# One row in eight of the query weights loaded over other queues: 112 rows on SP, two rows in sixteen parts, fourteen rows in two-row DMAs from GpSimd

## Chip, core and metric

The kernel runs on one NeuronCore of a Trainium2 chip. The metric is device time in microseconds (us), the median over runs; every time is that of one execution of the whole program. A core has four compute engines: TensorE (PE; its weight loads are PEld), VectorE (DVE), ScalarE (ACT) and GpSimd (POOL). SyncE (SP) here only issues DMAs. Sixteen DMA engines move all data between HBM and the core's memory (SBUF), whichever queue a DMA was issued on. A DMA is split into packets over these engines, and it has landed when the last of them is done.

## The reference

One decode step of a block that adds attention over a cache and a token-mixing MLP to its input. Batch 8, one token, width 512; 32 query heads share 8 key/value heads; 8192 cached positions of 128 numbers; float32 throughout.

```python
xn = _layernorm(x)
q = (xn @ wq).reshape(B, 1, 32, 128)                  # wq: 512 x 4096
scores = einsum(q, repeat(k_cache, 4)) * 128 ** -0.5
o = einsum(softmax(scores), repeat(v_cache, 4))
A = o.reshape(B, 1, 4096) @ wo                        # wo: 4096 x 512
h = _layernorm(xn)
u = gelu(einsum("bsd,sf->bdf", h, w1) + b1)           # 1792 features, S = 1
Bm = einsum("bdf,fs->bds", u, w2) + b2
return x + A + Bm.transpose(0, 2, 1)
```

Keys and values are 268 MB each, `wq` and `wo` 8.4 MB each. Every byte of them is used once.

## The kernel before

Work goes by pairs of one key/value head and one batch entry, `N_IT` = 64 in all. A pair has one key load (`raw<-in_A_k_cache_dram`) and one value load of 4 MB each. A load fills one of five slots (`RING`) of the tile `raw`: 128 partitions with 32 KB in each. `load_next` (L87) takes the next load from a list, `order`, and issues it on SP's queue; it is called as soon as the program has written the last use of a slot, so SP stands there until that use is over. All loads of the stream go through this one queue, in the list's order. The first key load is cut into four pieces of 8 KB a partition, and the last value load into five (`PIECES`), followed by the last part of `wo` in four pieces (L109).

For one pair, VectorE turns the keys in place in four quarters (`turn_keys`, L259), TensorE multiplies them with the placed queries (`qk`, L270), the softmax goes over VectorE, TensorE and ScalarE (L282 to L322), and TensorE multiplies with the values (`pv`, L337, and L347 for the last pair). `pair(i)` interleaves the keys of pair i, the scores of i-1 and the values of i-2. Between them ScalarE and GpSimd carry the MLP in 112 small steps (`mx_step`, L427 to L429), which read `w1t`, `b1t` and `w2t`. The last three pairs are written out by hand at the end, followed by the output projection `y_add` (L411), which reads the last part of `wo`, and the store of the result.

At the start the query weights `wq` come first on SP's queue. They take two slots: 128 partitions with 64 KB each, every partition one contiguous row of 64 KB in HBM (L83). Three loads follow at once: two of keys and one of values. The projection `q_project` (L224, matmuls at L230) reads all of `wq`; after it the two slots are free, and the next key and value load are issued. Before the projection stand the two layer norms, and a matmul (L218) that needs `b2t` through L210.

GpSimd's queue carries four small loads at the start: `w1t`, `b1t`, `w2t` (128 rows of 56 bytes each) and `b2t` (8 rows of 4 bytes). ACT's queue carries the input `x`. Near the end, in the last fifteen turns of the main loop, SP also issues a small DMA into `pad`, of 15 rows of 16 bytes in the first of these turns and one row less in each after it (L490). Nothing reads `pad`.

DMAs signal completion through semaphores, eight for SP's and ACT's queues together (`DMAHW0` to `DMAHW7`) and eight for GpSimd's (`DMASW0` to `DMASW7`), used in turn. A DMA whose semaphore is still in use by an earlier one waits for that one to land.

Of the kernel before, what the change touches and what calls it, by code (L numbers as in the profile page):

```python
# [14 lines left out]
B, D, HQ, HKV, SK, DH, F = 8, 512, 32, 8, 8192, 128, 1792  # L15
REP = HQ // HKV
P = 128
# [7 lines left out]
NC = D // P  # L25
# [3 lines left out]
N_IT = B * HKV  # L29
# [11 lines left out]
def attn_mixer_kernel(ctx: ExitStack, tc: tile.TileContext, x, kc, vc, wq, wo, w1, b1, w2, b2, out):  # L41
    nc = tc.nc
    place = ctx.enter_context(tc.tile_pool(name="place", bufs=1))
    pad = place.tile([P, PAD // 4], F32, name="pad")
# [4 lines left out]
    def slot(n=1):  # L49
        at = taken[0] % RING  # L50
        taken[0] += n
        return slots[:, at:at + n, :]
# [11 lines left out]
    def misc():  # L64
        return ps_m.tile([P, 512], F32, name="misc")
# [11 lines left out]
    at = [o[1:] for o in order].index((kc, KR, N_IT - 1))  # L77
    order[at], order[at + 1] = order[at + 1], order[at]
    WQ = []

    def load_wq():
        t = slot(2).rearrange("p s m -> p (s m)")
        nc.sync.dma_start(t, wq.rearrange("(p c) n -> p (c n)", c=NC))  # L83
        t = t.rearrange("p (c n) -> p c n", c=NC)
        WQ.extend(t[:, c, :] for c in range(NC))

    def load_next():  # L87
        if order:
            _, src, to, i = order.pop()
            h, b = divmod(i, B)  # L90
            t = slot().rearrange("p s (t d) -> p (s t) d", d=DH)
            rows = src[b, h].rearrange("(p t) d -> p t d", p=P)
            first, last = to is KR and not i, not order
            at = 0
            for n in (CH_T,) * NCH if first else PIECES if last else (NT,):
                nc.sync.dma_start(t[:, at:at + n, :], rows[:, at:at + n, :])
                at += n
            to[i] = t
            if last:
                load_wo(HKV - 1)  # L100
# [3 lines left out]
    def load_wo(h):  # L104
# [7 lines left out]
        wos[h] = t  # L112

    load_wq()
    early = one.tile([P, HB, 512], F32, name="ob")
    x_sb = early[:B, 0, :]
    nc.scalar.dma_start(x_sb, x.rearrange("b s d -> (b s) d"))
    w1t = const.tile([P, NF], F32, name="w1t")
    b1t = const.tile([P, NF], F32, name="b1t")
    w2t = const.tile([P, NF], F32, name="w2t")  # L120
    b2t = const.tile([B, 1], F32, name="b2t")
    yrow = const.tile([W, D], F32, name="yrow")
    for _ in range(RING - 2):
        load_next()
    nc.gpsimd.dma_start(w1t, w1.rearrange("s (p c) -> p (s c)", p=P))
    nc.gpsimd.dma_start(b1t, b1.rearrange("(p c) -> p c", p=P))
    nc.gpsimd.dma_start(w2t, w2.rearrange("(p c) s -> p (c s)", p=P))
    nc.gpsimd.dma_start(b2t, bass.AP(tensor=b2.tensor, offset=b2.offset, ap=[[0, B], [1, 1]]))
    quarter = [slice(j * D // NB, (j + 1) * D // NB) for j in range(NB)]


    ident = const.tile([P, P], F32, name="ident")
    make_identity(nc, ident)

# [46 lines left out]
    for k in range(NPT):  # L183
        t = const.tile([P, CH_T * W + W], F32, name=f"pt{k}")
# [3 lines left out]
    for k in range(2):  # L188
        t = const.tile([P, REP, W], F32, name=f"ot{k}")
        nc.gpsimd.memset(t, 0.0)  # L190
        OTS.append(t)


    def layer_norm(dst, src):
# [18 lines left out]
    m = misc()  # L213
# [3 lines left out]
    m = misc()  # L217
# [6 lines left out]
    def q_project():  # L224
        for a in range(2):
            m = misc()
            for c in range(NC):
                for g in range(HKV // 2):
                    o = (a * HKV // 2 + g) * REP * DH
                    nc.tensor.matmul(m[g * W:(g + 1) * W, :], xnT[:, c, :], WQ[c][:, o:o + REP * DH],  # L230
                                     start=(c == 0), stop=(c == NC - 1))
# [3 lines left out]
            for r in range(REP):  # L235
                nc.tensor.transpose(mt[:, r * P:(r + 1) * P], q[:, r * DH:(r + 1) * DH], ident)
            nc.vector.tensor_copy(QT[:, a * HKV // 2:(a + 1) * HKV // 2].rearrange("p g b r -> p r g b"),
                                  mt.rearrange("p (r g b) -> p r g b", r=REP, b=W)[:, :, :, :B])
        WQ.clear()
        load_next()  # L240
# [198 lines left out]
    def pair(i):  # L439
        h, b = divmod(i, B)  # L440
        k, v = i - 1, i - 2
        mb, mj = divmod(2 * (i - 1), NF)
        mixing = 0 <= mb < B
        turn_keys(i, 0)
        if k >= 0:
            qk(k)
        if v > 0:
            o_place(v - 1)
        if b == 0:
            q_place(h)  # L450
        turn_keys(i, 1)
        if k >= 0:
            sm_max(k)
            sm_spread(k)
        if v >= 0:
            pv(v, 0)
        if mixing:
            if mj == 0:
                if mb:
                    mx_end(mb - 1)  # L460
                mx_begin(mb)
            mx_step(mb, mj)
        if mb == B and mj == 0:
            mx_end(B - 1)
        turn_keys(i, 2)
        if k >= 0:
            sm_bias(k)
            sm_exp(k)
        if v >= 0:
            pv(v, 1)  # L470
            o_take(v)
        turn_keys(i, 3)
        if k >= 0:
            sm_send(k)
            if k >= N_IT - B:
                sm_sum(k)
            sm_turn(k)
        if mixing:
            mx_step(mb, mj + 1)
        if b == 3 and h:  # L480
            o_project(h - 1)
        if b == 3 and h < HKV - 1:
            load_wo(h)

    spare = pad[:16, :60].rearrange("p (n k) -> p n k", k=4)
    for i in range(N_IT - 2):
        pair(i)
        n = N_IT - 3 - i
        if 0 < n < 16:
            nc.sync.dma_start(spare[:n, n - 1, :], wo[:n, :4])  # L490


    k = N_IT - 1
# [88 lines left out]
```

## Time and profile before

| | |
|---|---|
| median of 3 runs | 1295.35 us (1294.91 to 1295.48) |
| the profiled execution, its own time | 1294.88 us |
| its span, first to last instruction | 1293.1 us |
| busy: PE / DVE / ACT / POOL | 829.3 / 726.9 / 331.2 / 229.6 us |
| read from HBM | 553.69 MB, 428 GB/s over the span |
| granted TensorE clock, mean | 0.818 |

The profile is of one execution. Its page has busy times, the span in 40 slices with the busy share of the 16 DMA engines, the DMA queues, the chain of waits followed back from the last instruction, and the costliest groups of instructions. q1 is SP's queue, q10 ACT's, q0 GpSimd's; q8 and q14 carry instructions, which the engines fetch while they run. A view of chosen stretches of time gives each engine's busy time in it (with the count of instructions), the granted clock, and the DMA share and rate. The timeline lists instructions as start, duration, engine, line, operation and names; in square brackets stands how long the engine was idle before, and what ended it. Engines are not told apart within the DMA share.

### The profile page before, as it was taken

How to read it: one execution, taken by the hardware profiler on the slowest of the kernel's cores; microseconds unless marked ns; L12 is line 12 of the kernel's file. 1: busy time of each engine (PE TensorE's matmuls, PEld its weight loads, DVE VectorE, ACT ScalarE, POOL GpSimd, SP SyncE). 2: the span in 40 equal slices, each digit the busy share in tenths (PEclk: the TensorE clock that was granted, in tenths of full speed). 3: DMA queues.
4: the chain of work that ended last, by engine and by line, in shares of the span. 5: the costliest groups of instructions: out<-in, count | busy, mean ns of one | idle time of the engine just before them, and what ended most of it. 6: DMA issues, size and time to landing. Idle time of an engine off the chain costs nothing.

```text
span 1293.1 us, 11759 instructions
## 1 busy us (share of the span) xinstructions
PE 829.3 (64%) x4890; PEld 244.5 (19%) x4890; DVE 726.9 (56%) x648; ACT 331.2 (26%) x479; POOL 229.6 (18%) x247
## 2 busy tenths in 40 slices
PE   2664766756757656666657576567564774657777
PEld 0111211211211111211112111121121221112223
DVE  2655456565555554654646556556456555556774
ACT  0232323222422313223233132232323232311000
POOL 1112112211212122121121131211211221110000
PEclk9877778878878788787887797787876887878899
DMA  9999999999999999999999999999999999999997
GB/s 407 426 432 436 430 435 432 432 432 434 431 432 433 433 432 431 436 431 430 434 431 433 433 430 435 431 433 433 432 431 431 435 432 428 435 432 430 433 437 315
DMA packets 21640, 554.45 MB, mean 429 GB/s; under 512 B 2732, under 2 KB 2764, under 8 KB 3540
## 3 DMA queue, kind: packets, MB, share of 16 engines
q1 hardware_dynamic: 21444, 553.68, 99.4%
q8 instruction: 38, 0.62, 0.2%
q14 instruction: 14, 0.11, 0.0%
q0 software_dynamic: 128, 0.02, 0.0%
q10 hardware_dynamic: 16, 0.02, 0.0%
HBM read 553.69 MB, written 0.02 MB: 428 GB/s over the span
## 4 chain that ended last, share of the span: by engine, by line
DMA 66%; PE 19%; DVE 14%; issue 1%; ACT 0%; SPq 0%; POOL 0%; ACTq 0%; DVEq 0%; POOLq 0%
DMA raw<-in_A_k_cache_dram 63%; PE acc L337 13%; DVE raw L259 12%; DMA raw<-in_A_v_cache_dram 2%; PE misc L287 2%; DMA b2t<-in_B_b_dram 2%; DVE mr L282 1%; PE acc L270 1%; PE misc L230 1%; PE misc L433 0%; PE misc L387 0%; PE hb L419 0%; PE misc L311 0%; DVE oc L366 0%; PE misc L218 0%
## 5 line engine op out<-in xcount | busy, mean ns | idle before, releaser
L259 DVE STREAM_TRANSPOSE raw<-raw 128x2048 f32<-128x2048 f32 x256 | 583.6, 2295 | 292.1 <-DMA raw<-in_A_k_cache_dram 292.1
L337 PE MATMUL acc<-raw,pt 128*32 128x512 f32 x2016 | 340.2, 829 | 0.0
L287 PE MATMUL misc<-ident,mr 128*128 128x128 f32 x128 | 47.0, 466 | 401.0 <-DVE mr L282 401.0
L270 PE MATMUL acc<-raw,z 128*32 128x512 f32 x2048 | 261.0, 609 | 9.7 <-DVE raw L259 7.6
L428 POOL TENSOR_SCALAR g<-g,w2t 128x512 f32<-128x512 f32 x112 | 77.7, 694 | 789.7 <-ACT g L427 789.7
L304 ACT ACT_TABLE_LOAD x57 | 73.1, 1283 | 333.8 <-DVE nb L293 333.5
L429 POOL TENSOR_TENSOR macc<-macc,g 128x512 f32<-128x512 f32 x112 | 142.3, 1271 | 9.4
L427 ACT ACTIVATE g<-hb,b1t,w1t 128x512 f32<-128x512 f32 x112 | 87.1, 777 | 219.7 <-PE hb L419 127.1
L322 DVE STREAM_TRANSPOSE pt<-misc 128x512 f32<-128x512 f32 x64 | 45.5, 710 | 140.0 <-PE misc L311 140.0
L337 PEld LDWEIGHTS acc<-raw,pt 128*32 128x32 f32 x2016 | 74.9, 145 | 211.5 <-issue 210.3
L287 PEld LDWEIGHTS misc<-ident,mr 128*128 128x128 f32 x128 | 29.4, 285 | 449.3 <-DVE mr L282 449.3
L304 ACT ACTIVATE t2k<-acc,nb 128x512 f32<-128x512 f32 x64 | 44.0, 688 | 233.4 <-DVE nb L293 232.8
L270 PEld LDWEIGHTS acc<-raw,z 128*32 128x32 f32 x2048 | 66.5, 111 | 186.3 <-issue 169.7
L311 PE MATMUL misc<-t2k,send 128*128 128x512 f32 x128 | 76.0, 677 | 23.4 <-ACT t2k L304 23.4
L427 ACT ACT_TABLE_LOAD x57 | 73.1, 1283 | 1.0
L358 ACT COPY ob<-acc 128x512 f32<-128x512 f32 x56 | 32.7, 584 | 98.9 <-PE acc L337 98.9
L387 PE MATMUL misc<-ob,pick 128*128 128x512 f32 x112 | 51.5, 603 | 0.0
L282 DVE TENSOR_REDUCE mr<-acc 128x1 f32<-128x512 f32 x64 | 41.8, 653 | 3.0 <-PE acc L270 3.0
L311 PEld LDWEIGHTS misc<-t2k,send 128*128 128x128 f32 x128 | 19.4, 191 | 78.4 <-issue 40.7
L434 DVE TENSOR_TENSOR yrow<-misc,yrow 32x512 f32<-32x512 f32 x8 | 5.4, 678 | 42.7 <-PE misc L433 42.7
L405 PE MATMUL misc<-wo,ot 128*32 128x512 f32 x56 | 27.0, 629 | 0.0
L421 POOL MEMSET macc<- 128x512 f32 x8 | 4.2, 525 | 116.4 <-PE misc L433 97.2
(90 smaller groups left out, 229.5 us busy)
## 6 DMA issues: line engine op xcount, KB each, us to landing
raw<-in_A_k_cache_dram SPq DMA_DIRECT2D x63, 4096.0 KB
raw<-in_A_v_cache_dram SPq DMA_DIRECT2D x63, 4096.0 KB
wo<-in_A_wo_dram SPq DMA_DIRECT2D x7, 1024.0 KB
raw<-in_A_k_cache_dram SPq DMA_DIRECT2D x4, 1024.0 KB
raw<-in_A_v_cache_dram SPq DMA_DIRECT2D x3, 1024.0 KB
raw<-in_A_v_cache_dram SPq DMA_DIRECT2D x2, 512.0 KB
wo<-in_A_wo_dram SPq DMA_DIRECT2D x4, 256.0 KB
ob<-in_A_x_dram ACTq DMA_DIRECT2D x1, 16.0 KB
```

Of the source, the lines that this page charges most:

```text
L259: nc.vector.transpose(k, k)
L270: nc.tensor.matmul(S[i][c * W:(c + 1) * W, :].rearrange("p (t j) -> p t j", j=W), Z[:, q, b, :], k[:, c * CH_T:(c + 1) * CH_T, q * W:(q + ...
L282: nc.vector.tensor_reduce(mr, S[i], AX.X, ALU.max)
L287: nc.tensor.matmul(m[:, :P], st[i].to_broadcast([P, P]), ident, start=True, stop=True)
L304: nc.scalar.activation(p, S.pop(i), AF.Exp, bias=st[i], scale=SCALE, accum_out=lr)
L311: nc.tensor.matmul(m, send, st[i][0], start=True, stop=True)
L322: nc.vector.transpose(PT[i % NPT][:, :CH_T * W], st.pop(i)[0])
L337: nc.tensor.matmul(O[i][j * W:(j + 1) * W, :].rearrange("p (c d) -> p c d", c=NCH), pt[:, t * W:(t + 1) * W], v[:, t], start=(t < NB), sto ...
L387: nc.tensor.matmul(m.rearrange("p (b d) -> p b d", b=HB), pick[:, c, :], ob[:, :, c * DH:(c + 1) * DH], start=(c == 0), stop=(c == NCH - 1))
L427: nc.scalar.activation(g, hb, AF.Gelu_apprx_tanh, bias=b1t[:, j:j + 1], scale=w1t[:, j:j + 1])
L428: nc.gpsimd.tensor_scalar(g, g, w2t[:, j:j + 1], 1.0, op0=ALU.mult, op1=ALU.mult)
L429: nc.gpsimd.tensor_add(acc, acc, g)
```

## The change

Partition rows 0 to 111 of `wq` stay one DMA on SP's queue. Rows 126 and 127 follow there as one DMA each, cut into sixteen parts of 4 KB. The other fourteen rows are issued from GpSimd's queue by `load_side`, two rows at a time: five DMAs of two whole rows and four of two half rows (`PAIRS` has first row, first and last half). Between some of them stand seven small DMAs of 2 to 15 rows of 16 bytes into `pad` (`BETWEEN`). `b2t` moves from GpSimd's queue to ACT's; `w1t`, `b1t` and `w2t` move behind GpSimd's memsets. The fifteen small DMAs on SP near the end go away.

```diff
     WQ = []
+    OWN = 112
+    SPRAYED = (126, 127)
+    PAIRS = ((112, 0, 2), (114, 0, 2), (116, 0, 1), (118, 0, 2), (120, 0, 2), (116, 1, 2), (122, 0, 2), (124, 0, 1), (124, 1, 2))
+    BETWEEN = {0: 15, 3: 2, 4: 6, 6: 4, 7: 6, 8: 6, 9: 7}
+    side = []
+
+    def load_side():
+        for x in range(len(side) + 1):
+            if x in BETWEEN:
+                n = BETWEEN[x]
+                o = 4 * sorted(BETWEEN).index(x)
+                nc.gpsimd.dma_start(pad[:n, o:o + 4], wq[:n, :4])
+            if x < len(side):
+                nc.gpsimd.dma_start(*side[x])
 
     def load_wq():
         t = slot(2).rearrange("p s m -> p (s m)")
-        nc.sync.dma_start(t, wq.rearrange("(p c) n -> p (c n)", c=NC))
+        rows = wq.rearrange("(p c) n -> p (c n)", c=NC)
+        n = NC * HQ * DH
+        nc.sync.dma_start(t[:OWN], rows[:OWN])
+        for p in SPRAYED:
+            nc.sync.dma_start(t[p:p + 1].rearrange("p (m w) -> p m w", m=16), rows[p:p + 1].rearrange("p (m w) -> p m w", m=16))
+        side.extend((t[p:p + 2, a * n // 2:e * n // 2], rows[p:p + 2, a * n // 2:e * n // 2]) for p, a, e in PAIRS)
...
-    nc.gpsimd.dma_start(w1t, w1.rearrange("s (p c) -> p (s c)", p=P))
-    nc.gpsimd.dma_start(b1t, b1.rearrange("(p c) -> p c", p=P))
-    nc.gpsimd.dma_start(w2t, w2.rearrange("(p c) s -> p (c s)", p=P))
-    nc.gpsimd.dma_start(b2t, bass.AP(tensor=b2.tensor, offset=b2.offset, ap=[[0, B], [1, 1]]))
+    nc.scalar.dma_start(b2t, bass.AP(tensor=b2.tensor, offset=b2.offset, ap=[[0, B], [1, 1]]))
...
     make_identity(nc, ident)
+    load_side()
...
         nc.gpsimd.memset(t, 0.0)
         OTS.append(t)
+    nc.gpsimd.dma_start(w1t, w1.rearrange("s (p c) -> p (s c)", p=P))
+    nc.gpsimd.dma_start(b1t, b1.rearrange("(p c) -> p c", p=P))
+    nc.gpsimd.dma_start(w2t, w2.rearrange("(p c) s -> p (c s)", p=P))
...
-    spare = pad[:16, :60].rearrange("p (n k) -> p n k", k=4)
     for i in range(N_IT - 2):
         pair(i)
-        n = N_IT - 3 - i
-        if 0 < n < 16:
-            nc.sync.dma_start(spare[:n, n - 1, :], wo[:n, :4])
```

What stands on SP's queue at the start of the program, before the change, with what each instruction waits for in brackets (a shape is rows by numbers per row, `x4` four alike in a row):

```order
L83 DMA raw<-in_A_wq_dram 128x16384
L96 DMA raw<-in_A_k_cache_dram 128x2048 x4
L96 DMA raw<-in_A_k_cache_dram 128x8192
L96 DMA raw<-in_A_v_cache_dram 128x8192
L96 DMA raw<-in_A_k_cache_dram 128x8192 [waits DMAHW1_49,DMAHW0_49,PE_49]
```

And with the change, at the same place:

```order
L99 DMA raw<-in_A_wq_dram 112x16384
L101 DMA raw<-in_A_wq_dram 1x16384 x2
L115 DMA raw<-in_A_k_cache_dram 128x2048 x3
L115 DMA raw<-in_A_k_cache_dram 128x2048 [waits DMAHW0_49]
L115 DMA raw<-in_A_k_cache_dram 128x8192 [waits DMAHW1_49]
L115 DMA raw<-in_A_v_cache_dram 128x8192 [waits DMAHW2_49]
```

There are three DMAs in place of one, and with more DMAs the semaphores come round sooner: the second key load (the row of 128x8192) now waits for `DMAHW1`, the semaphore of the 112-row load.

On GpSimd (POOL), before, behind the barrier at the program's start:

```order
L125 DMA w1t<-in_B_w_dram 128x14
L126 DMA b1t<-in_B_b_dram 128x14
L127 DMA w2t<-in_B_w_dram 128x14
L128 DMA b2t<-in_B_b_dram 8x1
masks.py:197 MEMSET ident 128x128
```

With the change, from the end of the making of `ident` on:

```order
L91 DMA pad<-in_A_wq_dram 15x4
L93 DMA raw<-in_A_wq_dram 2x16384 x2
L93 DMA raw<-in_A_wq_dram 2x8192
L91 DMA pad<-in_A_wq_dram 2x4
L93 DMA raw<-in_A_wq_dram 2x16384
L91 DMA pad<-in_A_wq_dram 6x4
L93 DMA raw<-in_A_wq_dram 2x16384
L93 DMA raw<-in_A_wq_dram 2x8192 [waits DMASW0_49]
L91 DMA pad<-in_A_wq_dram 4x4 [waits DMASW1_49]
```

Seven more follow, each waiting for the DMA eight places ahead of it to land; then the memsets, and `w1t`, `b1t` and `w2t`. The first eight are issued without a wait.

On TensorE, the first matmul of the projection, before and then with the change:

```order
L230 MATMUL misc<-raw,ob 32x512 [waits DMAHW1_49,DVE_49]
```

```order
L250 MATMUL misc<-raw,ob 32x512 [waits DMASW5_49,DMASW7_49,DMASW4_49,DMAHW1_49,DMASW3_49,DMAHW3_49,DMASW2_49,DMAHW4_49,DMASW1_49,DVE_49]
```

It waited for one DMA on `wq`; it now waits for the three of SP's queue and for GpSimd's.

## The prediction, made before the changed kernel had run

> **What bounds the kernel now.** I began with the page: span, DMA line, queues, chain of waits.
>
> ```profile
> span 1293.1 us, 11759 instructions
> DMA  9999999999999999999999999999999999999997
> q1 hardware_dynamic: 21444, 553.68, 99.4%
> q8 instruction: 38, 0.62, 0.2%
> q14 instruction: 14, 0.11, 0.0%
> DMA 66%; PE 19%; DVE 14%; issue 1%; ACT 0%; SPq 0%; POOL 0%; ACTq 0%; DVEq 0%; POOLq 0%
> ```
>
> The 16 DMA engines are busy in every slice but the last, and two thirds of the chain is DMA. Beside the 553.68 MB of data the same engines carry instruction fetches: 38 packets on q8, 0.62 MB, so 16 KB each. Next, the busy time by stretches of time: bulk, start, the end microsecond by microsecond.
>
> ```profile
> core 0: us, PE busy (x) PEld busy (x) DVE busy (x) ACT busy (x) POOL busy (x), PEclk, DMA share, GB/s
> 8.00:16.00 8.00, 0.61 (x4) 0.55 (x4) 3.90 (x16) 0.59 (x2) 0.00 (x0) 1.00 0.91 394
> 200.00:1200.00 1000.00, 641.19 (x3692) 186.65 (x3688) 562.40 (x474) 275.65 (x390) 193.37 (x200) 0.81 1.00 432
> 1281.00:1282.00 1.00, 1.00 (x36) 0.73 (x28) 0.41 (x1) 0.00 (x0) 0.00 (x0) 1.00 0.93 377
> 1282.00:1283.00 1.00, 1.00 (x31) 0.78 (x26) 0.97 (x2) 0.00 (x0) 0.00 (x0) 1.00 0.67 277
> 1283.00:1284.00 1.00, 0.97 (x26) 0.68 (x18) 0.46 (x2) 0.00 (x0) 0.00 (x0) 1.00 0.60 246
> 1284.00:1285.00 1.00, 0.88 (x32) 0.81 (x32) 0.17 (x1) 0.00 (x0) 0.00 (x0) 1.00 0.59 236
> 1285.00:1286.00 1.00, 0.84 (x24) 0.38 (x16) 0.00 (x0) 0.00 (x0) 0.00 (x0) 1.00 0.58 225
> 1286.00:1287.00 1.00, 0.36 (x14) 0.35 (x16) 0.00 (x0) 0.00 (x0) 0.00 (x0) 1.00 0.55 201
> 1287.00:1288.00 1.00, 0.59 (x14) 0.32 (x5) 0.29 (x1) 0.00 (x0) 0.00 (x0) 1.00 0.40 156
> 1288.00:1289.00 1.00, 0.74 (x25) 0.59 (x24) 0.17 (x1) 0.00 (x0) 0.00 (x0) 1.00 0.26 100
> ```
>
> In the bulk the share is 1.00 at 432 GB/s: 27 GB/s per engine, so a 64 KB row of the query weights costs its engine 65536 B / 27 = 2.43 us. At the end the engines do not stop together. By 1283 the share has dropped to 0.60, some nine or ten of 16; six or seven are done by about 1282. The others run on to about 1288.8. Every data load gives each engine the same bytes, so the late ones have done something else as well. The fetches are the candidate. This window of 1.2 us holds one:
>
> ```profile
> q8 instruction: 1, 0.02, 4.9%
> ```
>
> 4.9% of 16 engines over 1.2 us is 0.94 us. If eight engines carry the 38, each has 4.75, at least 4.5 us. The gap of 6 to 7 us then means about 1.4 us for a fetch with what it delays (6.5 x 8 / 38), an estimate from these rows.
>
> Last, the chain of waits and the timeline, for whether the end follows the late engines.
>
> ```profile
> 1205.17 23.26 DMA raw<-in_A_k_cache_dram
> 1228.46 2.31 DVE raw L259
> 1259.78 26.83 DMA raw<-in_A_v_cache_dram
> 1286.65 0.65 PE L347 MATMUL acc<-raw,pt 128*32 128x128 f32 x16 [0.64 <-DMA raw<-in_A_v_cache_dram]
> 1289.17 0.16 PEld L411 LDWEIGHTS hb<-wo,ot 128*32 128x32 f32 x8 [0.24 <-DMA wo<-in_A_wo_dram]
> ```
>
> It does. A load counts as landed when its slowest engine is done. VectorE waits for a key load until 1228.46; the compute from there runs almost without a stall, and the last value pieces and the last `wo` piece arrive 0.64 and 0.24 us after they are wanted. So landings that all move by some x move the end by x. If only the last pieces moved, about 1 us of it would count.
>
> **The change part by part.** *The rows.* Before, 128 rows of 64 KB are eight per engine. Now 112 are seven per engine, and two rows in sixteen parts add 2/16. The remaining fourteen go in nine two-row DMAs (five whole, four half) from GpSimd's queue. If such a DMA uses as many engines as it has rows, counted onward from where the last one stopped, the sixteen DMAs with the dummies between (15, 2, 6, 4, 6, 6 and 7 rows) work out from the tables as: four positions 2.5 rows, two 1.5, two 0.5, eight nothing. Net: eight engines -0.875 row = -2.13 us, two -0.375 = -0.91, two +0.625 = +1.52, four +1.625 = +3.95; the sum is zero. If the eight are the late ones, the last landing goes from 1288.8 to 1286.7; early engines near 1282 go to 1286 at most. That eight stay without a row, and about that many are late, fits; the views name no engine, so which eight remains an assumption.
>
> No placement can win more than this: the shares from 1281 to 1289 sum to 4.58 us of all sixteen, so a common end would be 1285.6, 3.2 us before 1288.8.
>
> *The extra packets.* The start, and the four GpSimd DMAs of before:
>
> ```profile
> q0 software_dynamic: 128, 0.02, 0.6%
> w1t<-in_B_w_dram POOLq DMA_DIRECT2D x1, 7.0 KB, 9.4
> b1t<-in_B_b_dram POOLq DMA_DIRECT2D x1, 7.0 KB, 13.5
> w2t<-in_B_w_dram POOLq DMA_DIRECT2D x1, 7.0 KB, 17.9
> b2t<-in_B_b_dram POOLq DMA_DIRECT2D x1, 0.0 KB, 20.0
> 1.27 0.78 POOL w1t L125
> 23.10 0.47 DVE L210 TENSOR_SCALAR macc<-ob,b2t 8x512 f32<-8x512 f32 x1 [10.20 <-DMA b2t<-in_B_b_dram]
> 25.47 5.82 PE L230 MATMUL misc<-raw,ob 128*32 128x512 f32 x32
> 34.58 0.33 SPq L96 DMA_DIRECT2D raw<-in_A_k_cache_dram  x1
> ```
>
> The q0 row is of 1 to 23 us: 0.6% of 16 x 22 us is 2.1 us for 128 packets, 16 ns each. Four DMAs made the 128, so one puts two on each engine. Sixteen add 32: at most 0.5 us, less since these packets are mostly shorter. The fifteen dummies taken from SP gave up to 15 pairs, back up to 0.5 us. I take +0.2, between -0.3 and +0.5. Issuing costs nothing: SP mostly waits for free slots.
>
> *When the weights are complete.* Issued from 1.27 on, 0.54 to 0.78 apart, the three table loads landed 4.9 us apart (10.7, 15.5, 20.5): two packets each, every one behind a 64 KB row. So about four of the sixteen land while the seven rows run, to about 20 us. The rest queue behind the 8 KB pieces of the first key load, 0.3 us each: 0.6 us a DMA, 7 us for twelve, plus 2.5 rows = 6 us. I take 33 us. If all sixteen went at 4.9, it would be 10.7 + 15 x 4.9 = 84 us; if all went at 0.6, about the 22 us of now (8.4 MB at the early 394 GB/s, and the start). The projection (L230) began at 25.47 because it waited for `b2t`, now on ACT's queue, so it slips by about 7.5 us. Behind it on SP stands the next key load, issued 9.1 us after its start. The three loads ahead, 12.6 MB or 29 us, keep the engines in work to about 51 us, the spared ones to 49. So it costs nothing while the weights are complete by 49 - 9.1 = 40 us.
>
> The compute's lag is then eaten by what VectorE now waits for keys:
>
> ```profile
> 63.08 4.50 DVE L259 STREAM_TRANSPOSE raw<-raw 128x2048 f32<-128x2048 f32 x2 [3.89 <-DMA raw<-in_A_k_cache_dram]
> 82.40 4.50 DVE L259 STREAM_TRANSPOSE raw<-raw 128x2048 f32<-128x2048 f32 x2 [5.30 <-DMA raw<-in_A_k_cache_dram]
> 101.73 4.50 DVE L259 STREAM_TRANSPOSE raw<-raw 128x2048 f32<-128x2048 f32 x2 [6.51 <-DMA raw<-in_A_k_cache_dram]
> ```
>
> 7.5 us is gone by the second such wait; later waits are as long. Without that cover each microsecond would show in the end.
>
> *The new wait on SP.* The second key load now stands behind a semaphore of the 112-row load (order above). That lands at 20 to 24 us; the first key load holds the engines 9.7 us longer, to 29.5. Nothing, with some 5 us spare. GpSimd's memsets and the three table loads now stand behind its sixteen DMAs. The memsets are first read after the projection. The tables are first read here:
>
> ```profile
> 53.31 0.78 ACT L427 ACTIVATE g<-hb,b1t,w1t 128x512 f32<-128x512 f32 x1 [11.80 <-PE hb L419]
> ```
>
> That is 28 us behind the projection's start, about 60 us with weights at 33; three loads of 4.9 us after 33 are in time.
>
> **Sum.** 1293.1 - 2.1 + 0.2 = 1291.2 us of span. The profiled execution took 1294.88, so 1.8 lies outside its span: 1293.0. The median of before, 1295.35, stands 0.5 over that execution: **1293.4 us**, 0.15% less. About 0.2%, 2.6 us, is what a measurement of this kernel can tell from no change, so the likeliest result is "same".
>
> **A rule, and a rival.** The trace shows only one GpSimd DMA under 16 rows, and not which engines it used. *Rival 1: the count does not move on.* If each two-row DMA starts at the same engine, fourteen rows land on two engines: 7 rows each, net +6.125 rows = +14.9 us. Were these early ones, they end at 1282 + 14.9 = 1296.9, 8.1 us after 1288.8: 1303.5; were they late, 1310. It decides as soon as four rows or so share an engine. For it: nothing here shows a moving count. Against: dummies of just these sizes only make sense with one. [...]
>
> *Rival 2: the count starts elsewhere* (an earlier program left it there, as `b2t`'s eight rows would). Then two or more late engines gain 0.625 to 1.625 rows, 1.5 to 3.9 us: 1296.9 to 1299.3.
>
> *Rival 3: a dry queue.* Weights complete at 84 instead of 40 us leave the engines idle for up to 44 us: up to 1339. Against: the pieces of the first key load are short, and 33 leaves 7 us.
>
> *Rival 4: it does not do what it says.* The rows are dealt evenly over 16: 1295.4. [...]
>
> *Rival 5: more than this*, towards the common end: 1292.2.
>
> **Chances.** Forecast 0.56, rival 1 0.12, rival 2 0.10, rival 3 0.07, rival 4 0.05, rival 5 0.10. Forecast alone: 1292.5 to 1294.3. Range: 1292.0 to 1299.0, which leaves out rivals 1 and 3. Faster by over 0.2% (under 1292.8): rival 5 and the forecast's low end, 0.18. Slower (over 1297.9): rivals 1, 3 and half of 2, 0.24. Same: 0.58.
>
> **What would show it.** Right: DMA shares near the end that fall later and more steeply, none left after about 1287; `L250` starting near 33 us; q1 and q0 bytes as cut; a key wait of nearly nothing at the first, back to 5 us by the third or fourth. Wrong: shares of 0.1 to 0.15 for many microseconds (rival 1), a slice of low DMA between 45 and 90 us (rival 3), an unchanged staircase (rival 4).

## The result, and the profile after

The changed kernel took **1344.74 us** (median of 5 runs, 1343.65 to 1345.55), the kernel before, beside it, 1294.93 us (median of 5, 1294.91 to 1295.48). The ratio is 1.0382, 95% interval 1.0367 to 1.0398: slower by 49.8 us, far outside the predicted range.

The page of the changed kernel (span, DMA share in 40 slices of 33.6 us, two queues, and the group of the projection's matmuls):

```profile
span 1343.7 us, 11776 instructions
DMA  9969999999999999999999999999999999999997
q1 hardware_dynamic: 21192, 552.76, 97.9%
q0 software_dynamic: 608, 0.94, 0.4%
L250 PE MATMUL misc<-raw,ob 128*32 128x512 f32 x64 | 10.1, 790 | 63.3 <-DMA raw<-in_A_wq_dram 63.3
```

The bytes moved as cut: 0.94 MB on GpSimd's queue, 14 of 64 KB and the small loads. One part of the change did something other than its code says. The page before and the page after count packets by size:

```profile
DMA packets 21640, 554.45 MB, mean 429 GB/s; under 512 B 2732, under 2 KB 2764, under 8 KB 3540
DMA packets 21884, 554.45 MB, mean 413 GB/s; under 512 B 2972, under 2 KB 3004, under 8 KB 3780
```

Between 2 and 8 KB there are 3540 - 2764 = 776 packets before and 3780 - 3004 = 776 after. Rows 126 and 127 in sixteen parts of 4 KB would have added 32. So they were not spread in such parts; the trace has 114 packets of 64 KB on SP's queue, 112 + 2, so each of the two rows went as one packet.

The loss stands at the start. The DMA share of the third slice is only 0.6 to 0.7, and the projection waited 63.3 us for the weights. Stretches of time tell more. Before the change (columns as in the prediction, the last two are DMA share and GB/s):

```profile
0.00:48.00 48.00, 19.74 (x104) 5.66 (x108) 19.77 (x38) 6.00 (x14) 5.84 (x16) 0.96 0.99 416
48.00:82.00 34.00, 22.34 (x124) 5.76 (x116) 19.46 (x16) 11.16 (x14) 8.74 (x10) 0.80 1.00 430
82.00:94.00 12.00, 6.47 (x36) 1.95 (x36) 9.71 (x7) 2.58 (x4) 1.06 (x1) 0.72 1.01 436
0.00:200.00 200.00, 113.86 (x630) 32.05 (x634) 104.36 (x106) 50.85 (x77) 36.18 (x48) 0.82 1.00 427
```

The same stretches of the changed kernel, and the next 200 us:

```profile
0.00:48.00 48.00, 2.52 (x6) 0.73 (x6) 7.75 (x31) 1.87 (x3) 6.81 (x16) 1.00 0.97 232
48.00:82.00 34.00, 0.00 (x0) 0.00 (x0) 0.00 (x0) 0.00 (x0) 7.56 (x15) 1.00 0.93 252
82.00:94.00 12.00, 10.25 (x68) 2.97 (x68) 0.40 (x1) 0.59 (x1) 0.00 (x0) 1.00 0.25 86
0.00:200.00 200.00, 76.25 (x438) 21.62 (x438) 70.21 (x78) 34.79 (x50) 35.99 (x53) 0.90 0.93 329
200.00:400.00 200.00, 129.31 (x732) 36.91 (x732) 115.39 (x97) 54.72 (x80) 38.42 (x40) 0.80 1.00 428
```

Read share and rate together. Until 82 us the engines are busy (0.97 and 0.93) but move little more than half of what they moved before: a busy engine is not always a moving one. From 82 to 94 they stand: 0.25. In time lost against before: 48 x (1 - 232/416) = 21.2 us, 34 x (1 - 252/430) = 14.1, 12 x (1 - 86/436) = 9.6; over the first 200 us 200 x (1 - 329/427) = 45.9. From 200 to 400 the rate is 428 where it was 432, another 1.9. Of the 50.6 us between the spans, 2.8 are left for the rest of the run and its end.

How slow the engines are at the start shows in the queues' view of the window from 2 to 14 us, packets, MB and share of 16 engines. Before, and then the changed kernel:

```profile
q1 hardware_dynamic: 71, 4.65, 91.8%
```

```profile
q1 hardware_dynamic: 42, 2.75, 100.5%
```

All these packets are 64 KB rows (4.65 MB / 71, 2.75 MB / 42). A row took 0.918 x 16 x 12 / 71 = 2.5 us before, and 1.005 x 16 x 12 / 42 = 4.6 us now, in this window. No row of GpSimd's had begun in that window. The timeline of the changed kernel, by issuing engine (start, duration, engine, line, names, and in brackets the idle time before and what ended it):

```profile
1.83 47.74 SPq L115 DMA_DIRECT2D raw<-in_A_k_cache_dram  x5
92.81 0.33 SPq L115 DMA_DIRECT2D raw<-in_A_k_cache_dram  x1
18.46 0.52 POOL L93 DMA_DIRECT2D raw<-in_A_wq_dram  x1 [11.92 <-DMA pad<-in_A_wq_dram]
32.13 0.52 POOL L91 DMA_DIRECT2D pad<-in_A_wq_dram  x1 [13.16 <-DMA raw<-in_A_wq_dram]
49.20 0.52 POOL L93 DMA_DIRECT2D raw<-in_A_wq_dram  x1 [16.54 <-DMA raw<-in_A_wq_dram]
83.04 6.50 PE L250 MATMUL misc<-raw,ob 128*32 128x512 f32 x32 [63.28 <-DMA raw<-in_A_wq_dram]
```

SP stood before the second key load until about 49 us: the 112-row load, expected at 20 to 24 us, landed there. GpSimd waited 12 to 17 us for single landings. The projection began at 83.04 us, and the key load behind it was issued at 92.81, where 34.58 had been.

### The profile page after: what moved, and what is told of

The parts are those of the page before. It is cut to its first block, busy times and chain, and to the rows that moved or that the text cites. A ratio compares the mean times of both kernels' runs of the same rounds, so it can differ in the third digit from the quotient of the medians.

```text
span 1343.7 us, 11776 instructions
## 1 busy us (share of the span) xinstructions
PE 826.4 (61%) x4890; PEld 244.2 (18%) x4890; DVE 725.9 (54%) x648; ACT 331.0 (25%) x479; POOL 238.2 (18%) x262
## 2 busy tenths in 40 slices
DMA packets 21884, 554.45 MB, mean 413 GB/s; under 512 B 2972, under 2 KB 3004, under 8 KB 3780
## 4 chain that ended last, share of the span: by engine, by line
DMA 66%; PE 19%; DVE 13%; issue 1%; another core or an unknown queue 0%; ACT 0%; POOL 0%; SPq 0%; DVEq 0%; POOLq 0%; ACTq 0%
DMA raw<-in_A_k_cache_dram 58%; PE acc L357 13%; DVE raw L279 11%; DMA raw<-in_A_wq_dram 6%; PE acc L290 2%; DMA raw<-in_A_v_cache_dram 2%; PE misc L307 2%; DVE mr L302 1%; PE misc L250 1%; PE misc L453 0%; PE misc L407 0%; PE misc L331 0%; DVE oc L386 0%; PE hb L439 0%
## 5 line engine op out<-in xcount | busy, mean ns | idle before, releaser
L357 PE MATMUL acc<-raw,pt 128*32 128x512 f32 x2016 | 332.9, 813 | 0.0
L290 PE MATMUL acc<-raw,z 128*32 128x512 f32 x2048 | 266.6, 621 | 9.9 <-DVE raw L279 7.9
L250 PE MATMUL misc<-raw,ob 128*32 128x512 f32 x64 | 10.1, 790 | 63.3 <-DMA raw<-in_A_wq_dram 63.3
```

The lines of the kernel that those rows point to most:

```text
L290: nc.tensor.matmul(S[i][c * W:(c + 1) * W, :].rearrange("p (t j) -> p t j", j=W), Z[:, q, b, :], k[:, c * CH_T:(c + 1) * CH_T, q * W:(q + ...
L357: nc.tensor.matmul(O[i][j * W:(j + 1) * W, :].rearrange("p (c d) -> p c d", c=NCH), pt[:, t * W:(t + 1) * W], v[:, t], start=(t < NB), sto ...
```

## The experiments

Each is one execution with a profile; the kernel before took 1294.7 to 1294.9 us beside them, so differences of some us are plain. Three theories on the slow rows, all three suppositions (no view shows which engine carries a row): **W**, on the write side: engines that write the same part of SBUF at one time share that part's rate, and how a DMA's rows are dealt over the engines decides it; **R**, on the read side: the distance of the rows in HBM; **Q**: only GpSimd's queue is slow. Loads left unnamed are as before.

**sp112**: the kernel before, its weights cut in two on SP.

```diff
-        nc.sync.dma_start(t, wq.rearrange("(p c) n -> p (c n)", c=NC))
+        nc.sync.dma_start(t[:112], rows[:112])
+        nc.sync.dma_start(t[112:], rows[112:])
```

> Before, with the query weights on SP alone as one DMA of 112 rows and one of 16 rows; GpSimd's queue as before. Theory W (write side: a DMA of 112 rows is dealt so that engines write the same part of SBUF at one time): rows of 64 KB take about 4.7 us as in the changed kernel, the 112 rows 33 us in place of 17, and the time rises by 16 us or more, to 1311 to 1325. Theory R (read side: rows that engines read at one time lie badly in HBM): the same. Theory Q (only the rows on GpSimd's queue slow the engines): rows take 2.4 us and the time stays at 1295.

Measured 1314.86 us, span 1313.1: 20.0 us over the span before, with none of the weights on GpSimd's queue. The first 48 us, and SP's queue while the 112 rows went out (1 to 29.5 us) and while the sixteen did (29.5 to 35.5):

```profile
0.00:48.00 48.00, 3.76 (x14) 1.12 (x18) 8.55 (x31) 1.87 (x3) 5.91 (x16) 1.00 0.96 230
q1 hardware_dynamic: 112, 7.34, 104.7%
q1 hardware_dynamic: 32, 1.05, 133.5%
```

That is about the 232 GB/s of the changed kernel. Q can't be the whole: cutting the load is enough for 20 us. Both parts of the cut cost. The 112 rows took 1.047 x 16 x 28.5 / 112 = 4.3 us each, the sixteen (the other 16 packets are tiny) 1.335 x 16 x 6 / 16 = 8.0 us, against 2.5 before: for each engine 7 x 1.8 = 12.6 us and 5.5 us, some 18 of the 20.0.

**sp16x8**: the weights as eight DMAs of 16 neighbouring rows, on SP.

```diff
+        for o in range(0, P, 16):
+            nc.sync.dma_start(t[o:o + 16], rows[o:o + 16])
```

> Before, with the query weights as eight DMAs of 16 rows on SP, one row an engine: the sixteen engines write sixteen neighbouring partitions at a time. W: more engines share a part of SBUF than with 112 rows, so rows take longer than 4.7 us, up to 9.7 if four engines share, and the time rises by 20 to 58 us, to 1315 to 1353. R: sixteen rows read at one time lie in one stretch of 1 MB, no reason for slowness: 1295 to 1300. Q: 1295 to 1300.

Measured 1349.75 us (span 1348.0, +54.9). The first 48 us, and SP's queue while the rows went out (1 to 71 us):

```profile
0.00:48.00 48.00, 0.62 (x4) 0.55 (x4) 7.82 (x27) 1.87 (x3) 5.24 (x15) 1.00 1.01 114
q1 hardware_dynamic: 240, 8.39, 105.4%
```

All sixteen engines are busy and move 114 GB/s, about a quarter of 432. The 128 rows took 1.054 x 16 x 70 / 128 = 9.2 us each; eight rows on each engine at 9.2 in place of 2.5 are 53.6 us, nearly the whole loss.

**dst128_pitch448** and **dst112_pitch256** part R from W. The first keeps one DMA of 128 rows but reads them 112 KB apart from the key cache; the second keeps 112 rows and 16 but reads the 112 at 36.5 KB. Both project other numbers, so their results are not those of the block.

```diff
+        nc.sync.dma_start(t, bass.AP(tensor=kc.tensor, offset=kc.offset, ap=[[n * 7 // 4, P], [1, n]]))
...
+        nc.sync.dma_start(t[:112], bass.AP(tensor=wq.tensor, offset=wq.offset, ap=[[9344, 112], [1, n]]))
+        nc.sync.dma_start(t[112:], rows[112:])
```

> [...] W: rows take 2.4 us, the time stays at 1295. R: rows take about 4.7 us, the time rises by about 19 us to 1314.

> [...] W: rows take about 4.7 us and the time is that of the run with 112 and 16 rows. R: rows take 2.4 us, about 1295 to 1300.

Measured 1295.65 and 1317.05 us. A new distance in HBM costs 0.7 us with 128 rows (415 GB/s over the first 48 us, where before ran at 416), and the 112 rows stay slow with another distance (217 GB/s, where sp112 ran at 230). R falls for these loads.

**sp16x8_step8** parts W from "a DMA of few rows is slow": sixteen rows a DMA, as in sp16x8, but others.

```diff
+        for o in range(8):
+            nc.sync.dma_start(t[o::8], rows[o::8])
```

> The kernel before with the query weights as eight DMAs of 16 rows on SP, as in sp16x8, but each takes every eighth row (0, 8, 16 ... 120) instead of 16 neighbours. Rows, bytes and DMAs are the same; only which partitions are written at one time differs. [...] Theory that a DMA of few rows is slow as such: 1349 again, with 9.3 us. [...]

Measured 1318.76 us, where neighbours took 1349.75. The first 24 us, SP's queue while the rows went out (1 to 39 us), and a stretch around the end of the weights:

```profile
0.00:24.00 24.00, 0.61 (x4) 0.55 (x4) 7.06 (x27) 1.87 (x3) 5.38 (x15) 1.00 1.06 220
q1 hardware_dynamic: 240, 8.39, 106.6%
36.00:48.00 12.00, 4.00 (x24) 1.22 (x28) 0.00 (x0) 0.00 (x0) 0.00 (x0) 1.00 0.68 173
```

220 GB/s, in place of 114, from nothing but the choice of rows. A row took 1.066 x 16 x 38 / 128 = 5.1 us. Eight on each engine are 8 x 2.6 = 20.8 us of the 23.9 in the span; the engines that stood from 36 to 48 us (12 x (1 - 0.68) = 3.8 us) are about the rest, as SP issued the first key load only at 43.93. Few rows in a DMA can't be the reason for the 9.2, as there are as few here. The row price is 3.7 times that of before with neighbours and twice with every eighth row, as if four engines, or two, shared the rate of one. W fits this, by an estimate from these prices: sixteen engines sharing by fours would make four parts of 114 / 4 = 28.5 GB/s, sharing by twos eight parts of 220 / 8 = 27.5, both near the 432 / 16 = 27 of one engine in the bulk. That rows share anything on the write side, and which rows would, no run shows directly; it stays the author's estimate. One rival is left: the choice of rows also sets how far apart they lie in HBM (64 or 512 KB). Another distance cost 0.7 us with 128 rows, but no run changes it for sixteen rows alone.

**after_nodummy**: the changed kernel without its seven small DMAs (`BETWEEN = {}`).

> The changed kernel without the seven small DMAs between the GpSimd rows. If a two-row GpSimd DMA always goes to the same two engines (the count does not move on), the small DMAs place nothing: 1338 to 1346 us, the fourteen rows still one after another on two engines, L250 still starting near 83. If the count moves on, nine two-row DMAs spread over all sixteen engines: the weights are complete near 50, and the time falls to 1315 to 1325.

Measured 1345.05 us: the same. GpSimd's issues, a late stretch, and the projection:

```profile
1.46 5.05 POOL L93 DMA_DIRECT2D raw<-in_A_wq_dram  x8 [0.15 <-issue]
20.58 0.52 POOL L93 DMA_DIRECT2D raw<-in_A_wq_dram  x1 [14.07 <-DMA raw<-in_A_wq_dram]
83.00:85.00 2.00, 1.30 (x12) 0.58 (x12) 0.34 (x1) 0.58 (x1) 0.00 (x0) 1.00 0.11 45
77.58 5.69 PE L250 MATMUL misc<-raw,ob 128*32 128x512 f32 x32 [55.05 <-DMA b1t<-in_B_b_dram]
```

All nine row DMAs were issued by 21 us, yet the projection began only at 77.58 (the releaser named is not the one that counts: `b1t` is no input of this line). The small DMAs change nothing in the time. Late, the share is 0.11 to 0.13, two engines of sixteen (0.125): they work off what is left while fourteen stand. In the changed kernel's trace never more than two of GpSimd's eighteen row packets are under way at one time.

**after_one14**: the fourteen rows as one DMA of fourteen rows, no small DMAs.

```diff
+    PAIRS = ((112, 0, 2),)
+        side.extend((t[p:p + 14, a * n // 2:e * n // 2], rows[p:p + 14, a * n // 2:e * n // 2]) for p, a, e in PAIRS)
```

> The changed kernel with the fourteen rows as one GpSimd DMA of fourteen rows and no small DMAs. Theory that the fourteen rows cost on top of the 112-row load because they stand on two engines: one DMA of fourteen rows spreads over fourteen engines, and the time falls to what the 112-row load alone cost, 1315 to 1322. Theory that GpSimd's queue itself is slow beside SP's: 1335 or more.

Measured 1318.63 us: 26.1 below the changed kernel, 3.8 above sp112. GpSimd's queue from 8 to 16 us, and the stretch that moved 252 GB/s in the changed kernel:

```profile
q0 software_dynamic: 16, 0.92, 94.2%
48.00:82.00 34.00, 20.96 (x116) 6.19 (x116) 15.81 (x10) 4.12 (x11) 0.00 (x0) 0.95 1.01 423
```

The fourteen rows (0.92 MB) took 0.942 x 16 x 8 / 14 = 8.6 us each, near the 9.2 of sixteen neighbours, but all fourteen at once: the same rows on the same queue cost little once fourteen engines carry them. The projection began at 54.46. From 48 to 82 us the rate is 423 GB/s, and after_nodummy moved 243 there, so the slow stretch goes with the two-row DMAs. By what way they slow the other engines, busy at a share of 0.93, no run shows.

**after_k0one**: the changed kernel with the first key load in one piece, so that SP no longer waits for the 112-row load.

```diff
-            for n in (CH_T,) * NCH if first else PIECES if last else (NT,):
+            for n in PIECES if last else (NT,):
```

> The changed kernel with the first key load in one piece, so that the second key load and the value load no longer wait on SP for the 112-row load to land. If that wait costs (it was given some 5 us to spare, and the 112-row load landed at 47.8 us), some us less: 1337 to 1342. If the engines had work anyway until then: 1343 to 1346.

A miss: 1353.32 us, 8.6 slower. SP, the projection, and three stretches:

```profile
1.83 1.05 SPq L115 DMA_DIRECT2D raw<-in_A_k_cache_dram  x2
93.47 3.64 PE L250 MATMUL misc<-raw,ob 128*32 128x512 f32 x16 [73.91 <-DMA raw<-in_A_wq_dram]
76.00:80.00 4.00, 0.00 (x0) 0.00 (x0) 0.00 (x0) 0.00 (x0) 2.44 (x5) 1.00 0.12 49
84.00:88.00 4.00, 0.00 (x0) 0.00 (x0) 0.00 (x0) 0.00 (x0) 0.75 (x2) 1.00 0.12 50
92.00:96.00 4.00, 2.53 (x12) 0.68 (x16) 0.00 (x0) 0.00 (x0) 0.00 (x0) 1.00 0.13 57
```

The wait is gone: all early loads are issued by 3.5 us. But the weights come 10 us later, and in these stretches between 76 and 96 us two engines work alone. The wait had kept the second key load and the value load off those two engines; without it their packets go out between the weights' rows. That is my reading of these lines; it has no run of its own.

**control**: all of the change but the rows (one DMA of 128 rows on SP; `b2t` on ACT's queue, the tables behind the memsets, no small DMAs near the end).

> All of the change but the rows: the query weights in one DMA of 128 rows on SP, b2t on ACT's queue, w1t, b1t and w2t behind the memsets, no small DMAs near the end. All theories: within 1 us of the kernel before, 1294 to 1296, so that the whole loss belongs to the rows. Above 1298, one of the moved small loads costs.

Measured 1294.90 us beside 1294.71: those edits cost nothing.

**cols128, cols16x8, cols2x64** cut the weights by columns: SP 14336 numbers of all 128 rows, GpSimd the last 2048, in one DMA, eight, or 64 (`step` is 128, 16 or 2; no small DMAs).

```diff
+        m = n * 7 // 8
+        nc.sync.dma_start(t[:, :m], rows[:, :m])
+        side.extend((t[p:p + step, m:], rows[p:p + step, m:]) for p in range(0, P, step))
```

> The changed kernel with the weights cut by columns in place of rows: SP loads the first 14336 numbers of all 128 rows, GpSimd the last 2048 (8 KB) of all 128 rows in one DMA; no small DMAs. Theory that only the dealing of the rows costs: both DMAs are dealt as before, 1294 to 1296. Theory that GpSimd's queue, or weights split over two queues, costs: 1298 or more.

> As cols128, with GpSimd's part in eight DMAs of 16 neighbouring rows. The same bytes on the same queue, differently dealt. Theory of shared parts: an 8 KB piece takes four times 0.3 us, eight of them on each engine, about 7 us more before the weights are complete, and all engines are held up alike: 1299 to 1304. If dealing does not matter: as cols128.

> As cols128, with GpSimd's part in 64 DMAs of two rows. Theory that a two-row DMA from GpSimd always goes to the same two engines: 64 pieces of 8 KB each on two engines, two engines on one part of SBUF: 64 x 0.6 = 37 us beside their 17 us of SP's rows, weights complete at 55 to 80 us, and what is beyond the engines' cover of 49 us is lost: 1303 to 1330, with L-lines of the projection starting then. If the count moved on, the pieces would spread over all engines: 1296 to 1304.

Measured 1294.68, 1301.66 and 1335.68 us: the same 1 MB on the same queue, and only the dealing differs. The first, beside 1294.75 for the kernel before, shows that a second queue is free. The second costs 7 us, as expected from W, but not by the price expected. GpSimd's queue in cols16x8 from 6 to 32 us:

```profile
q0 software_dynamic: 289, 1.06, 14.4%
```

Its 128 pieces took at most 0.144 x 16 x 26 / 128 = 0.47 us each, where I had said four times 0.3. The first 48 us ran at 350 GB/s where cols128 ran at 415, 7.5 us, but not by that working: that the size came out was luck. The third is beyond what I expected; its projection, one stretch with GpSimd's queue in it, and two landings:

```profile
29.87 2.78 PE L249 MATMUL misc<-raw,ob 128*32 128x512 f32 x24
89.69 1.94 PE L249 MATMUL misc<-raw,ob 128*32 128x512 f32 x8 [57.04 <-DMA raw<-in_A_wq_dram]
48.00:82.00 34.00, 0.00 (x0) 0.00 (x0) 0.00 (x0) 0.00 (x0) 12.16 (x24) 0.50 0.45 181
q0 software_dynamic: 909, 0.42, 4.3%
58.61 0.52 POOL L93 DMA_DIRECT2D raw<-in_A_wq_dram  x1 [2.26 <-DMA raw<-in_A_wq_dram]
61.66 0.52 POOL L93 DMA_DIRECT2D raw<-in_A_wq_dram  x1 [2.53 <-DMA raw<-in_A_wq_dram]
```

Only the last eight matmuls need the late columns, and they wait until 89.69. GpSimd, eight DMAs ahead, gets one landing in about 3 us: were the pairs on different engines, several of the eight would land in that time. So the pairs stand one behind another on the same two engines, by my reading with SP's packets between them. That pace, which I had not priced, is the miss; the doubled time for two engines on one part, 0.6 us, which I had, was not what set it: the 51 pieces of this stretch (0.42 MB) took at most 0.043 x 16 x 34 / 51 = 0.46 us each, which is 0.7 of one engine's time in it.

No kernel here beat the one before; cols128 and control are level with it.

## Why the prediction was wrong

**The step that failed** is the rows' term: "Net: eight engines -0.875 row = -2.13 us". It rested on "a 64 KB row of the query weights costs its engine 65536 B / 27 = 2.43 us", read from loads of 128 rows, and took that price over to loads of 112 and of 2. The measured price was 4.6 us in the first rows of the changed kernel's 112-row load, 4.3 over the whole of sp112's, and 8.0 in the sixteen rows behind it. Cutting the load alone made sp112 20.0 us slower, and 21.2 us of the changed kernel's loss lie in its first 48 us. No rival of mine had it: I counted rows per engine, never which rows the engines write at one time. That the choice of rows sets the price is shown for sixteen rows (9.2 or 5.1 us each); that it does so on the write side is the author's estimate, for the 112 rows too.

**The counting** in the same term, "counted onward from where the last one stopped", was wrong too. Rival 1 was right in its mechanism, fourteen rows on two engines: never more than two of their packets under way at once, and a share of 0.10 to 0.15 of sixteen from 84 to 92 us. It was mis-sized, 8.1 to 14.9 us at the end of the run; the rows' cost over the one 14-row DMA is 1344.74 - 1318.63 = 26.1 us. The 49.8 us thus come in three steps: 19.9 to sp112, 3.8 more to after_one14, 26.1 more to the changed kernel. The harm of the last was done at the start: the two engines hold back the weights, so the next loads, and the other fourteen stand (a share of 0.25 from 82 to 94 us). The dummies "only make sense" with a moving count, I wrote; after_nodummy takes the same time without them. That "two rows in sixteen parts add 2/16" failed too: each of these rows went as one packet of 64 KB. What that cost has no run of its own. The count that moves on, from which the -2.13 us were worked out, no run shows; the runs showed two-row DMAs one behind another on two engines in its place.

**"I take 33 us"** for the complete weights came out at 83. The upper end, 84, was nearly met, but by another way: not sixteen DMAs at 4.9 us each, but seven rows in series on each of two engines. The price for that, up to 44 us of idle engines, was rival 3 with 0.07. It held in kind: a slice of low DMA share between 45 and 90 us was its sign, and it is there. As the engines were slow as well, only 9.6 us of the loss were such standing between 82 and 94.

**The SP wait**: "Nothing, with some 5 us spare". The 112-row load landed some 25 us later than that, so the wait was long. Still it cost nothing on balance: taking it away made things worse by 8.6 us. I had looked only at the wait's own harm, not at what it may keep out.

**Right**: the extra edits (`b2t`, the tables, the small DMAs of SP) at near nothing, control within 0.2 us of the kernel before; a second queue for weights at nothing, cols128; the bulk at 432 GB/s, the same from 400 to 1200 us.

**The end of the run.** I named "shares near the end that fall later and more steeply" as a sign of success. The changed kernel shows the steepness:

```profile
1333.00:1334.00 1.00, 1.00 (x30) 0.79 (x23) 0.95 (x2) 0.00 (x0) 0.00 (x0) 1.00 0.59 229
1335.00:1336.00 1.00, 1.00 (x30) 0.97 (x30) 0.17 (x1) 0.00 (x0) 0.00 (x0) 1.00 0.15 59
1338.00:1339.00 1.00, 0.52 (x10) 0.30 (x2) 0.32 (x2) 0.00 (x0) 0.00 (x0) 1.00 0.07 27
```

From 0.59 it falls to 0.15 in two microseconds, where before it stayed near 0.58 for three; then about one engine's share (0.0625) is left until 1339. It saved nothing. The engines had just stood idle together, and between 200 and 400 us they moved 428 GB/s where the kernel before moved 432; early engines that wait lose their lead. This I argue and did not test. Nor did any run show whether relieving the late engines would shorten the end. If W holds, doing it by moving rows promises little, as a row still goes to the same place in SBUF whichever engine carries it. This too is the author's estimate.

Open: how a 112-row DMA is dealt, row by row. Its 4.3 us a row lies between the 2.5 of the one load of 128 rows and the 5.1 of sp16x8_step8.

## What to carry to other kernels

A price per row or byte holds for the shape of the load it was measured in: before cutting a 128-partition DMA by rows, ask which partitions will be written at one time (sixteen neighbours ran at 114 GB/s, every eighth at 220); the cut by columns (cols128) cost nothing, 1294.68 us beside 1294.75. A split written in the program need not be one in the packets (a row in sixteen parts went as one of 64 KB), so count them by size. A DMA share of about 1.00 says only that engines are busy (1.01 stood beside 114 GB/s in sp16x8, 1.00 beside 432 in the bulk), so read GB/s beside it. And a wait is not a cost until the run without it is faster (after_k0one was 8.6 us slower): it may hold back work that competes with what is late.

## What was unexpected in the hardware

- Loads of equal bytes and equal row counts ran at 114 or 220 GB/s by the choice of rows alone (sixteen neighbours, or every eighth).
- A 112-row load with one of sixteen rows behind it ran at 230 GB/s over the first 48 us, where the kernel before, with one load of 128 rows, ran at 416: 20 us for a cut that looks harmless.
- Two-row DMAs from GpSimd went one behind another on two engines (a share of 0.11 to 0.13 when only they worked), with or without small DMAs between them, and held up the whole stream: 26.1 us more than the same rows in one DMA.
- A load of one row, written in the program as sixteen parts of 4 KB, went as a single packet of 64 KB.
